# A fused attention and max-out MoE kernel: early pieces of the first copies, a new order of loads at the start, and one score tile per pair moved into the MoE's accumulator banks

## The chip, the cores and the metric

One core of one Trainium2 chip. The metric is the device time of one launch in microseconds (us), lower is better.

## The reference

Block-wise causal attention (blocks of 64 tokens) on 8 batches, 8 heads, 576 tokens, head size 64; its result, 4608 tokens of 512, goes through two matrices of 512x1024, an elementwise maximum, and one of 1024x512.

```python
def _attn_ref(q, k, v):                      # each (8, 8, 576, 64)
    scores = scale * np.matmul(q, k.transpose(0, 1, 3, 2))
    mask = block_i >= block_j                # blocks of 64 tokens
    scores = np.where(mask, scores, -1000000000.0)
    attn = np.exp(scores - max); attn = attn / sum
    return np.matmul(attn, v)

def _moe_ref(x, w1, w2, w_out):              # x (4608, 512)
    g = np.maximum(x @ w1, x @ w2)           # (4608, 1024)
    return g @ w_out
```

## The kernel before

The program is scheduled by hand: each engine runs its instructions in the order in which they are written. Attention works on pairs of heads, two pairs to a group, 16 groups; 64-row matmuls for scores and transposes run two at a time on the halves of the array (in the trace the two of a pair start 0.003 us apart). MoE matmuls of 128 rows fill in between: `fill(n)` issues n of them. Accumulators lie in PSUM: the pool `ps_s` has two score buffers of two banks each, the pool `ps_m` four single banks, which h units, y units, attention output (`av`) and transposes share in rotation. An h unit makes 128 columns of g for up to 512 tokens, a y unit the final output of 128 tokens; `x_out` transposes the attention output into the MoE's input.

```python
def h_unit(i, f):                            # 8 matmuls, two banks of ps_m
    for w_sb in (w1_sb, w2_sb):
        pt = ps_m.tile([P, SPAN], FP32, name="ps_h", tag="m")
        for c in range(NDM):
            nc.tensor.matmul(pt[:, :w], w_sb[:, c, ...], xT[:, c, t0:t0 + w], ...)
            if c == NDM - 1:
                if not ph:
                    nc.vector.tensor_copy(out=h1[:, :w], in_=pt[:, :w])       # frees bank 1
                else:
                    nc.vector.tensor_max(g[:, f, m:m + w], h1[:, :w], pt[:, :w])  # frees bank 2
            yield                            # (bookkeeping cut)

def tile_0(p):                               # tile_1, tile_2 alike: 2 halves x 512 columns
    u = ps_s.tile([P, 2, 512], FP32, name="ps_s", tag="s")
    scores(p, u, 0, 0, 0, 512)
    return lambda: (exp(p, u, 512, 0), mask(p, 0))
# ... cut ...
for g in range(GPB, NG):                     # the steady loop, as before
    region(tile_0(a), tile_1(a))             # block of 64-row matmuls 1
    for p, tiles in ((a, lambda: (tile_2(a), tile_0(b))), (b, lambda: (tile_1(b), tile_2(b)))):
        fill(hi); av_with(p - LAG, lo)       # MoE and attention output
        copy_out = t_pair(p); outs = tiles() # blocks 2 and 3, with transposes
        copy_out(); region(*outs)
```

Loads of weights and v are issued by GpSimd, which also casts group 2's q and k; loads of q and k are issued by the sync engine.

The softmax here doesn't subtract the row's maximum and nothing guards it: scores larger than these inputs give would overflow.

Of the kernel before, what the change touches and what calls it, by code (L numbers as in the profile page):

```python
# [8 lines left out]
FP32 = mybir.dt.float32  # L9
BF16 = mybir.dt.bfloat16  # L10
AF = mybir.ActivationFunctionType
# [3 lines left out]
def kernel(  # L15
# [10 lines left out]
    nc = tc.nc  # L26
# [84 lines left out]
    def load_qk(g, queues, gated=False):  # L111
        b, u = divmod(g, GPB)
        for nm, src, queue in (("q", q, queues[0]), ("k", k, queues[1])):
            if queue is None:
                continue
            raws[nm, g] = t = raw.tile([P, 2, RPP * D], FP32, name=f"{nm}raw")
            if gated:
                nc.gpsimd.memset(t[:, 0, :1], 0.0)
            queue.dma_start(
                out=t[:],  # L120
                in_=src[b, 4 * u:4 * u + 4].rearrange(
                    "(s h) (p t) d -> (h p) s (t d)", h=2, t=RPP),
            )

    def cast(nm, g, parts):
        t = raws.pop((nm, g)).rearrange("p s (t d) -> p t s d", d=D)
        qk_n[nm, g] = n = qkn.tile([P, RPP, 2, D], BF16, name=f"{nm}n")
        for copy, j0, j1 in parts:
            copy(out=n[:, j0:j1], in_=t[:, j0:j1])  # L129
# [12 lines left out]
    def load_w(f0, fw, which=(0, 1)):  # L142
        for i in which:
            dst, src = ((w1_sb, w1r), (w2_sb, w2r))[i]
            nc.gpsimd.dma_start(out=dst[:, :, f0:f0 + fw], in_=src[:, :, f0:f0 + fw])
# [11 lines left out]
    nc.vector.memset(zeros[:], 0.0)  # L157
    nc.scalar.activation(out=warm[:], in_=warm[:], func=AF.Exp)
    load_qk(1, (SP, SP))
    load_qk(2, (SP, None))  # L160
    make_identity(nc, ident)
    for r in range(NV):
        nc.vector.memset(vv_r[r][:, :, :, D:D + 1], 1.0)
# [9 lines left out]
    load_w(0, 256, (0,))  # L173
    cast("k", 1, ((pool, 0, RPP),))
    load_w(0, 256, (1,))
    load_qk(2, (None, SP), gated=True)


    done_tokens = [0]
# [88 lines left out]

    plan()
    steps = [(u, need, cost) for u, need, cost, n in units for _ in range(n)]  # L270
    at = [0]


# [4 lines left out]
            n += 1  # L278
        return int(total)

    def fill(n):
        while n > 0 and at[0] < len(steps) and steps[at[0]][1] <= done_tokens[0]:
            u, _, cost = steps[at[0]]
            next(u)
            n -= cost
            at[0] += 1


    def warm_up(n):
        pw = ps_m.tile([P, SPAN], FP32, name="ps_w", tag="m")  # L290
        for _ in range(n):
            nc.tensor.matmul(pw[:], zeros[:, :P], zeros[:], start=True, stop=True)  # L292
# [4 lines left out]
    def transposes(nm, g, copies):  # L297
        n = qk_n.pop((nm, g))
        pts = [ps_m.tile([P, RPP, NP], BF16, name=f"ps_{nm}T", tag="m") for _ in range(2)]
        for j in range(RPP):  # L300
            for i in range(2):
                r = slice(i * NP, (i + 1) * NP)
                nc.tensor.transpose(  # L303
                    pts[i][:, j, :], n[r, j].rearrange("p s d -> p (s d)"), ident[r, r],
                )

        def copy_out(which=(0, 1)):
            for i in which:
                t = (qT_r if nm == "q" else kT_r)[(2 * g + i) % NT]
                copies[i](  # L310
                    out=t[:, :S].rearrange("q (p j) -> q p j", j=RPP),
                    in_=pts[i].rearrange("q j p -> q p j"),
                )
        return copy_out

# [11 lines left out]
    def pad_keys(p):  # L327
        nc.gpsimd.tensor_copy(
            out=kz_r[p % NT].rearrange("p (a c) -> p a c", c=BLK)[:, 0:3:2],
            in_=kT_r[p % NT][:, S - 3 * BLK:].rearrange("p (a c) -> p a c", c=BLK)[:, 0:3:2],  # L330
        )


    def corner_scores(p, ps, col):
# [25 lines left out]
    def burst_p(p):  # L360
        burst(p, ((0, 0, QCUT), (1, P, QCUT - P)), 0)

    def burst_q1(p):
        burst(p, ((0, QCUT, 320), (1, QCUT, 192)), 384)

    def burst_q2(p):
        burst(p, ((1, 448, P), (2, QCUT, 320), (4, 512, BLK)), 896)
# [4 lines left out]
    def masks_p(p, eng=None):  # L372
        for a in (0, 256):
            mask(p, a, eng)
# [34 lines left out]
    def region(*tiles):  # L409
        for out in tiles:  # L410
            out()

    def av(p, ts):
        b, hp = divmod(p, HP)
        vv = vv_r[b % NV]
        a = aT_r[p % NA]
        n = len(ts)
        h0 = hp // 2 * 4 + hp % 2
        if p % 2 == 0 and ts[0] == 0:
            xps[p // 2] = xpool.tile([P, NCH, 2, 2, D], BF16, name="xp")  # L420
        xp = xps[p // 2]
        po = ps_m.tile([P, n, 2, D + 1], FP32, name="ps_o", tag="m")
        n_mm = 2 * sum(t + 1 for t in ts)
        mm = 0
        for gi, t in enumerate(ts):
            for hh in range(2):
                for c in range(t + 1):
                    a0 = a_col(p, c, t)
                    nc.tensor.matmul(  # L429
                        po[:, gi, hh, :], a[:, hh, a0:a0 + P], vv[:, c, h0 + 2 * hh, :],  # L430
                        start=(mm == 0), stop=(mm == n_mm - 1),
                    )
                    mm += 1
        rec = small.tile([P, 3, 2, 1], FP32, name="rec")
        nc.vector.reciprocal(rec[:, :n, :, 0], po[:, :, :, D])  # L435
        nc.vector.tensor_mul(  # L436
            xp[:, ts[0]:ts[0] + n, :, p % 2], po[:, :, :, :D],
            rec[:, :n].to_broadcast([P, n, 2, D]),
        )

    def x_out(g, t0=0, t1=NCH):
        b, u = divmod(g, GPB)
        xp = xps[g]
        n = t1 - t0
        n_odd = min(t1, NCH - 1) - t0
        pe = ps_m.tile([P, 2, n, BLK], BF16, name="ps_xe", tag="m")
        po = ps_m.tile([P, 2, n_odd, BLK], BF16, name="ps_xo", tag="m")
        for s in range(2):
            for t in range(t0, t1):
                src = xp[:, t, s].rearrange("p a d -> p (a d)")  # L450
                nc.tensor.transpose(pe[:, s, t - t0, :], src[:BLK], ident[:BLK, :BLK])  # L451
                if t < NCH - 1:
                    nc.tensor.transpose(po[:, s, t - t0, :], src[BLK:], ident[BLK:, BLK:])
        dst = xT[:, 2 * u:2 * u + 2, b * S + t0 * P:b * S + t1 * P].rearrange(
            "p s (t h w) -> p s t h w", h=2, w=BLK)
        nc.vector.tensor_copy(out=dst[:, :, :, 0], in_=pe[:])  # L456
        nc.vector.tensor_copy(out=dst[:, :, :n_odd, 1], in_=po[:])
        if u == GPB - 1:
            done_tokens[0] = min(b * S + t1 * P, (b + 1) * S)

# [37 lines left out]
        return lambda: [f() for f in outs]  # L498


    warm_up(16)
    cq = transposes("q", 0, (dve, act))
    ck = transposes("k", 0, (act, dve))
    cq((0,))
    ck((0,))
    cq((1,))
    ck((1,))
    cast("q", 1, ((dve, 0, RPP),))
    burst_p(0)
    masks_p(0)  # L510
    burst_p(1)
    warm_up(2)
    masks_p(1)
    for c in range(2, NCH):
        load_v(0, c)
    load_w(256, 256)
    cq = transposes("q", 1, (dve, dve))
    burst_q1(0)
    ck = transposes("k", 1, (dve, dve))
    for i in range(2):  # L520
        cq((i,))
        ck((i,))
    load_w(512, 512)
    warm_up(3)
    burst_p(2)
    av(0, [0, 1])
    burst_q3(0)
    warm_up(2)
    burst_p(3)
    masks_p(2, nc.vector)  # L530
    av(1, [0, 1])
    masks_p(3, nc.vector)
    burst_q2(0)
    av(2, [0, 1])
    warm_up(2)
    burst_q1(1)
    av(3, [0, 1])
    x_out(0, 0, 2)
    warm_up(2)
    cast("q", 2, ((pool, 0, RPP),))  # L540
    masks_q(0)
    cast("k", 2, ((pool, 0, RPP),))
    burst_q2(1)
    x_out(1, 0, 2)
    warm_up(2)
    burst_q3(1)
    masks_q(1)
    for c in range(3):
# [39 lines left out]

    for g in range(GPB, NG):
        a, b = 2 * g, 2 * g + 1  # L590
        if x_due:
            x_out(x_due.pop())
        n = fill_of(g)
        region(tile_0(a), tile_1(a))
        if g == GPB:
            av(3, [2, 3, 4])
            fill(5)
            x_out(1, 2, NCH)
            n = fill_of(g)
        lo, hi = max(3, n // 18), n * 2 // 9  # L600
        for p, tiles in ((a, lambda: (tile_2(a), tile_0(b))), (b, lambda: (tile_1(b), tile_2(b)))):
            fill(hi)
            if g > GPB:
                av_with(p - LAG, lo)
            else:
                fill(lo)
            copy_out = t_pair(p)
            outs = tiles()
            copy_out()
            region(*outs)  # L610
            if p % 2 and g + 1 < NG:
                pad_keys(p + 1)
                pad_keys(p + 2)
            pool_work(p)
        if g > GPB:
            x_due.append(g - 1)
        fill(n - 2 * (lo + hi))
    for p in range(NPAIR - LAG, NPAIR):
        if x_due:
            x_out(x_due.pop())  # L620
# [40 lines left out]
```

## Time and profile before

| | before |
|---|---|
| time, median (4 runs, one of them slow) | 283.05 us (282.59 to 287.41) |
| TensorE busy | 96% |
| steady group | 15.0 us, three 64-row blocks |
| first h matmul | 18.09 us |

First, GpSimd's timeline (columns: start, duration, engine, line, what, how many in a row, and in brackets the idle time ahead with what ended it):

```profile
10.25 0.75 POOL L145 DMA_DIRECT2D w_sb<-in_moe_w_dram  x1
...
11.73 2.44 POOL L133 DMA_DIRECT2D vv<-in_v_dram  x3
14.15 3.01 POOL L145 DMA_DIRECT2D w_sb<-in_moe_w_dram  x4
17.20 1.14 POOL L129 CAST qn<-qraw 128x1152 bf16<-128x1152 f32 x1
```

It starts the cast of group 2's q at 17.20. Second, TensorE's timeline shows where the loop proper begins: the first full score tile, at 27.06.

```profile
27.06 0.61 PE L321 MATMUL ps_s<-qT,kT 64*128 64x512 bf16 x6
```

### The profile page before, as it was taken

Reading aid. Unit: us, or ns where it says so; the run is one execution under the profiler, and the core shown is the slowest. Engines: PE = TensorE matmul, PEld = TensorE weight load, DVE = VectorE, ACT = ScalarE, POOL = GpSimd, SP = SyncE. Lnnn points to the kernel's source line nnn. Section 1 sums busy time; section 2 is a strip of 40 time slices with the busy share of each in tenths; the row PEclk is TensorE's granted clock in tenths of the full one; section 3 lists DMA queues with packets and bytes.
Section 4 is the critical chain, followed back from the end, with each engine's and each line's share of the span. In section 5 each row is a group of like instructions: output and inputs, shape, how many; then the busy total and the mean of one; then the engine's idle time right before and its main releaser. Section 6 shows DMA issues by size and latency. Waiting matters only on the chain.

```text
span 280.4 us, 7767 instructions
## 1 busy us (share of the span) xinstructions
PE 269.3 (96%) x3208; PEld 151.5 (54%) x3253; DVE 185.7 (66%) x386; ACT 139.6 (50%) x194; POOL 107.7 (38%) x271
## 2 busy tenths in 40 slices
PE   7699999999999999999999999999999999999995
PEld 2356766655556455555555554646455644444543
DVE  5967879668887676767667576757655766365430
ACT  3786577667664664655647374664653000100112
POOL 2996446764654625164344625371120000000000
PEclk9999999999999999999999999999999999999999
DMA  7999999979934994479266866175301111111114
GB/s 261 263 219 220 187 244 273 250 148 189 210 42 153 154 156 78 178 82 239 49 208 77 219 75 196 52 81 50 67 5 49 49 54 40 39 75 40 73 41 150
DMA packets 55940, 36.68 MB, mean 131 GB/s; under 512 B 38752, under 2 KB 43232, under 8 KB 55904
## 3 DMA queue, kind: packets, MB, share of 16 engines
q0 software_dynamic: 41728, 7.87, 35.0%
q1 hardware_dynamic: 13760, 27.66, 28.8%
q10 hardware_dynamic: 416, 0.66, 0.7%
q8 instruction: 25, 0.41, 0.6%
q14 instruction: 11, 0.09, 0.1%
HBM read 34.60 MB, written 9.44 MB: 157 GB/s over the span
## 4 chain that ended last, share of the span: by engine, by line
PE 91%; DMA 4%; issue 2%; ACT 1%; DVE 1%; POOL 0%; ACTq 0%
PE ps_h L197 43%; PE ps_y L215 22%; PE ps_o L429 11%; PE ps_s L321 8%; DMA vv<-in_v_dram 2%; PE ps_xe L451 2%; PE ps_qT L303 2%; DMA qraw<-in_q_dram 2%; PE ps_kT L303 2%; ACT aT L345 1%; PE ps_s L339 1%; PE ps_y L231 1%; PE ps_w L292 1%; DVE g L206 0%; POOL vv L133 0%
## 5 line engine op out<-in xcount | busy, mean ns | idle before, releaser
L197 PE MATMUL ps_h<-xT,w_sb 128*128 128x512 bf16 (+3 forms) x605 | 136.2, 357 | 1.7 <-issue 0.3
L345 ACT ACTIVATE aT<-ps_s 128x1024 bf16<-128x1024 f32 (+2 forms) x100 | 96.2, 996 | 17.2 <-PE ps_s L321 16.2
L197 PEld LDWEIGHTS <-w_sb 128*128 128x128 bf16 x640 | 57.8, 98 | 57.4 <-issue 8.1
L204 DVE CAST h<-ps_h 128x512 bf16<-128x512 f32 (+3 forms) x80 | 50.9, 637 | 28.9 <-PE ps_h L197 26.7
L215 PE MATMUL ps_y<-wo_sb,g 128*128 128x512 bf16 x273 | 65.5, 379 | 2.1 <-PE ps_s L321 1.3
L206 DVE TENSOR_TENSOR g<-h,ps_h 128x512 bf16<-128x512 bf16 (+3 forms) x80 | 50.6, 632 | 12.0 <-PE ps_h L197 10.5
L350 POOL MEMSET aT<- 64x128 bf16 x124 | 22.3, 199 | 92.7 <-ACT aT L345 91.3
L221 ACT COPY y<-ps_y 128x512 f32<-128x512 f32 x31 | 18.1, 584 | 70.3 <-PE ps_y L215 56.5
L429 PEld LDWEIGHTS <-aT 128*128 128x128 bf16 x960 | 37.3, 98 | 14.1 <-issue 1.3
L215 PEld LDWEIGHTS <-g 128*128 128x128 bf16 x280 | 26.8, 98 | 30.4 <-issue 1.1
L429 PE MATMUL ps_o<-vv,aT 128*128 128x65 bf16 x960 | 39.9, 194 | 0.3 <-DMA vv<-in_v_dram 0.3
L133 POOL DMA_DIRECT2D vv<-in_v_dram x40 | 33.7, 847 | 0.5
L436 DVE TENSOR_TENSOR xp<-ps_o,rec 128x256 bf16<-128x256 f32 (+1 forms) x64 | 31.4, 491 | 2.2
L321 PE MATMUL ps_s<-qT,kT 64*128 64x64 bf16 (+6 forms) x344 | 31.6, 279 | 1.1 <-ACT kT L310 0.7
L435 DVE RECIPROCAL rec<-ps_o 128x4 f32<-128x4 f32 (+1 forms) x64 | 12.0, 188 | 20.6 <-PE ps_o L429 18.9
L310 ACT COPY qT<-ps_qT 128x576 bf16<-128x576 bf16 x15 | 9.6, 638 | 29.4 <-PE ps_qT L303 29.4
L187 POOL COPY g<-g 128x512 bf16<-128x512 bf16 x8 | 4.9, 611 | 38.3 <-DVE g L206 38.2
L129 POOL CAST kn<-kraw 128x1152 bf16<-128x1152 f32 x15 | 17.3, 1151 | 5.2 <-DMA kraw<-in_k_dram 5.1
L129 POOL CAST qn<-qraw 128x1152 bf16<-128x1152 f32 (+1 forms) x15 | 16.5, 1099 | 7.0 <-DMA qraw<-in_q_dram 6.9
L456 DVE COPY xT<-ps_xe 128x640 bf16<-128x640 bf16 (+2 forms) x18 | 8.2, 453 | 15.7 <-PE ps_xe L451 14.9
L310 ACT COPY kT<-ps_kT 128x576 bf16<-128x576 bf16 x15 | 9.6, 638 | 15.0 <-PE ps_kT L303 15.0
L321 PEld LDWEIGHTS <-kT 64*128 64x128 bf16 x344 | 13.2, 95 | 6.6 <-issue 2.8
(44 smaller groups left out, 144.5 us busy)
## 6 DMA issues: line engine op xcount, KB each, us to landing
qraw<-in_q_dram SPq DMA_DIRECT2D x16, 576.0 KB, 4.1
out_dram<-y SPq DMA_DIRECT2D x35, 256.0 KB, 2.1
kraw<-in_k_dram SPq DMA_DIRECT2D x15, 576.0 KB, 5.4
vv<-in_v_dram POOLq DMA_DIRECT2D x32, 128.0 KB, 5.3
w_sb<-in_moe_w_dram POOLq DMA_DIRECT2D x4, 256.0 KB, 6.6
w_sb<-in_moe_w_dram POOLq DMA_DIRECT2D x2, 512.0 KB, 10.7
wo_sb<-in_moe_w_out_dram POOLq DMA_DIRECT2D x2, 512.0 KB, 11.8
kraw<-in_k_dram ACTq DMA_DIRECT2D x1, 576.0 KB, 5.4
```

The lines of the kernel that those rows point to most:

```text
L129: copy(out=n[:, j0:j1], in_=t[:, j0:j1])
L133: nc.gpsimd.dma_start(out=vv_r[b % NV][P - rows:, c, :, :D], in_=v[b, :, c * P:c * P + rows, :].rearrange("h p d -> p h d"),)
L197: nc.tensor.matmul(pt[:, :w], w_sb[:, c, f * P:(f + 1) * P], xT[:, c, t0:t0 + w], start=(c == 0), stop=(c == NDM - 1),)
L204: nc.vector.tensor_copy(out=h1[:, :w], in_=pt[:, :w])
L206: nc.vector.tensor_max(g[:, f, m:m + w], h1[:, :w], pt[:, :w])
L215: nc.tensor.matmul(py[:], g[:, f, s * P:(s + 1) * P], wo_sb[:, f, :], start=(f == 0), stop=(f == NFF - 1),)
L310: copies[i](out=t[:, :S].rearrange("q (p j) -> q p j", j=RPP), in_=pts[i].rearrange("q j p -> q p j"),)
L321: nc.tensor.matmul(ps[:, hh, col:col + w], kT[r, k0:k0 + P], qT[r, q0:q0 + w], start=True, stop=True,)
L345: nc.scalar.activation(out=aT_r[p % NA][:, :, a0:a0 + w], in_=ps[:, :, :w], func=AF.Exp, scale=scale,)
L350: (eng or nc.gpsimd).memset(aT_r[p % NA][BLK:, :, a0:a0 + BLK], 0.0)
L429: nc.tensor.matmul(po[:, gi, hh, :], a[:, hh, a0:a0 + P], vv[:, c, h0 + 2 * hh, :], start=(mm == 0), stop=(mm == n_mm - 1),)
L436: nc.vector.tensor_mul(xp[:, ts[0]:ts[0] + n, :, p % 2], po[:, :, :, :D], rec[:, :n].to_broadcast([P, n, 2, D]),)
```

## The change

Two ideas. At the **start**, the columns of the transposed q and k that the first scores need are copied first (`LOW`), the rest behind (`HIGH`), partly on ScalarE; the weight blocks are loaded ahead of the rest of v, the last weights in two blocks of 256 columns instead of one of 512; group 2's q is loaded later, with its k. In the **loop**, tile 0 of each pair goes into two of the four MoE banks, so that all three tiles of a pair fit into one 64-row block: two blocks a group instead of three, and fewer switches between 64-row and 128-row mode. For that, `fill` gets a second argument that runs MoE units to their end before a block, so that whole banks come free, and in the loop `x_out`'s even copy goes to ScalarE; neither is in the cut below.

```diff
-    load_qk(2, (SP, None))                  # group 2's q, early
...
-    load_qk(2, (None, SP), gated=True)
+    load_qk(2, (SP, SP), gated=True)
...
+    def tile_0m(p):
+        us = [ps_m.tile([P, 512], FP32, name="ps_s0", tag="m") for _ in range(2)]
+        for hh in (1, 0):
+            nc.tensor.matmul(us[hh][:], kT_r[p % NT][r, :P], qT_r[p % NT][r, :512], ...)
+        def out():
+            for hh in range(2):
+                nc.scalar.activation(out=aT_r[p % NA][:, hh, :512], in_=us[hh][:], func=AF.Exp, scale=scale)
...                                           # the start
-    cq((0,)); ck((0,)); cq((1,)); ck((1,))
+    cq((0,), LOW); ck((0,), LOW); ck((1,), LOW); cq((1,), LOW); cq((0,), HIGH) ...
+    load_w(256, 256)
     for c in range(2, NCH):
         load_v(0, c)
-    load_w(256, 256)
...
-    burst_q1(0)                              # ahead of group 1's k transposes
...
-    load_w(512, 512)
+    load_w(512, 256)
+    load_w(768, 256)
...
+    x_out(0, 0, 2, (act, act))               # was behind the later scores, on VectorE
+    burst_q1(0)                              # now behind x_out(0)
...                                           # the loop, pair a; pair b has t_pair first
+                out1 = tile_1(a); out0 = tile_0m(a); out2 = tile_2(a)
+                copy_out = t_pair(a)
+                out0(); out1(); copy_out(); out2()
```

More of the change, by code (lines that the diff above doesn't have):

```diff
@@ L270 @@
     steps = [(u, need, cost) for u, need, cost, n in units for _ in range(n)]
+    inside = [j % (NDM if n > NFF or n == 2 * NDM and u.__name__ == "h_unit" else NFF) > 0
+              for u, _, _, n in units for j in range(n)]
     at = [0]
@@ L279, in ready, with fill @@
         return int(total)
-    def fill(n):
-        while n > 0 and at[0] < len(steps) and steps[at[0]][1] <= done_tokens[0]:
+    def fill(n, whole=False):
+        while at[0] < len(steps) and steps[at[0]][1] <= done_tokens[0]:
+            if n <= 0 and not (whole and inside[at[0]]):
+                break
             u, _, cost = steps[at[0]]
@@ L305, in transposes, with copy_out @@
                 )
-        def copy_out(which=(0, 1)):
+        def copy_out(which=(0, 1), part=(0, NP), copy=None):
+            p0, p1 = part
             for i in which:
                 t = (qT_r if nm == "q" else kT_r)[(2 * g + i) % NT]
-                copies[i](
-                    out=t[:, :S].rearrange("q (p j) -> q p j", j=RPP),
-                    in_=pts[i].rearrange("q j p -> q p j"),
+                (copy or copies[i])(
+                    out=t[:, p0 * RPP:p1 * RPP].rearrange("q (p j) -> q p j", j=RPP),
+                    in_=pts[i][:, :, p0:p1].rearrange("q j p -> q p j"),
                 )
@@ L331, in pad_keys @@
         )
+    def tile_0m(p):
+        us = [ps_m.tile([P, 512], FP32, name="ps_s0", tag="m") for _ in range(2)]
+        for hh in (1, 0):
+            r = slice(hh * D, (hh + 1) * D)
+            nc.tensor.matmul(
+                us[hh][:], kT_r[p % NT][r, :P], qT_r[p % NT][r, :512], start=True, stop=True)
+        def out():
+            for hh in range(2):
+                nc.scalar.activation(
+                    out=aT_r[p % NA][:, hh, :512], in_=us[hh][:], func=AF.Exp, scale=scale)
+            mask(p, 0)
+        return out
     def corner_scores(p, ps, col):
@@ L439, in av, with x_out @@
         )
-    def x_out(g, t0=0, t1=NCH):
+    def x_out(g, t0=0, t1=NCH, copies=(dve, dve)):
         b, u = divmod(g, GPB)
@@ L455, in x_out @@
             "p s (t h w) -> p s t h w", h=2, w=BLK)
-        nc.vector.tensor_copy(out=dst[:, :, :, 0], in_=pe[:])
-        nc.vector.tensor_copy(out=dst[:, :, :n_odd, 1], in_=po[:])
+        copies[0](out=dst[:, :, :, 0], in_=pe[:])
+        copies[1](out=dst[:, :, :n_odd, 1], in_=po[:])
         if u == GPB - 1:
@@ L498, in t_pair @@
         return lambda: [f() for f in outs]
+    LOW = (0, -(-QCUT // RPP))
+    HIGH = (LOW[1], NP)
     warm_up(16)
@@ L503 @@
     ck = transposes("k", 0, (act, dve))
-    cq((0,))
-    ck((0,))
-    cq((1,))
-    ck((1,))
+    cq((0,), LOW)
+    ck((0,), LOW)
+    ck((1,), LOW)
+    cq((1,), LOW)
+    cq((0,), HIGH)
     cast("q", 1, ((dve, 0, RPP),))
@@ L510 @@
     masks_p(0)
+    cq((1,), HIGH)
+    ck((0,), HIGH)
     burst_p(1)
+    ck((1,), HIGH)
     warm_up(2)
     masks_p(1)
+    load_w(256, 256)
     for c in range(2, NCH):
         load_v(0, c)
-    load_w(256, 256)
-    cq = transposes("q", 1, (dve, dve))
-    burst_q1(0)
-    ck = transposes("k", 1, (dve, dve))
-    for i in range(2):
-        cq((i,))
-        ck((i,))
-    load_w(512, 512)
-    warm_up(3)
-    burst_p(2)
-    av(0, [0, 1])
-    burst_q3(0)
-    warm_up(2)
-    burst_p(3)
-    masks_p(2, nc.vector)
-    av(1, [0, 1])
-    masks_p(3, nc.vector)
-    burst_q2(0)
-    av(2, [0, 1])
-    warm_up(2)
-    burst_q1(1)
-    av(3, [0, 1])
-    x_out(0, 0, 2)
-    warm_up(2)
-    cast("q", 2, ((pool, 0, RPP),))
+    cq = transposes("q", 1, (dve, act))
+    ck = transposes("k", 1, (dve, dve))
+    cq((0,), LOW)
+    cq((1,), LOW)
+    ck((0,), LOW)
+    ck((1,), LOW)
+    cq((0,), HIGH, act)
+    cq((1,), HIGH, dve)
+    load_w(512, 256)
+    load_w(768, 256)
+    warm_up(2)
+    burst_p(2)
+    ck((0,), HIGH, act)
+    av(0, [0, 1])
+    masks_p(2, nc.vector)
+    burst_p(3)
+    av(1, [0, 1])
+    ck((1,), HIGH, act)
+    masks_p(3, nc.vector)
+    warm_up(1)
+    av(2, [0, 1])
+    x_out(0, 0, 2, (act, act))
+    warm_up(1)
+    av(3, [0, 1])
+    burst_q1(0)
+    warm_up(1)
+    x_out(1, 0, 2, (dve, dve))
+    burst_q2(0)
+    warm_up(1)
+    cast("q", 2, ((pool, 0, RPP),))
+    fill(2)
+    burst_q3(0)
     masks_q(0)
     cast("k", 2, ((pool, 0, RPP),))
+    burst_q1(1)
+    fill(1)
     burst_q2(1)
-    x_out(1, 0, 2)
-    warm_up(2)
+    fill(1)
     burst_q3(1)
@@ L590 @@
         a, b = 2 * g, 2 * g + 1
-        if x_due:
-            x_out(x_due.pop())
         n = fill_of(g)
-        region(tile_0(a), tile_1(a))
-        if g == GPB:
-            av(3, [2, 3, 4])
-            fill(5)
-            x_out(1, 2, NCH)
-            n = fill_of(g)
-        lo, hi = max(3, n // 18), n * 2 // 9
-        for p, tiles in ((a, lambda: (tile_2(a), tile_0(b))), (b, lambda: (tile_1(b), tile_2(b)))):
-            fill(hi)
+        fill(0, True)
+        for p in (a, b):
+            if p == a and x_due:
+                x_out(x_due.pop(), copies=(act, dve))
+                n = fill_of(g)
+            if p == a:
+                out1 = tile_1(a)
+                out0 = tile_0m(a)
+                out2 = tile_2(a)
+                copy_out = t_pair(a) if g > GPB else (lambda: None)
+                out0()
+                out1()
+                copy_out()
+                out2()
+            else:
+                copy_out = t_pair(b)
+                out1 = tile_1(b)
+                out0 = tile_0m(b)
+                out2 = tile_2(b)
+                copy_out()
+                out1()
+                out0()
+                out2()
+                if g + 1 < NG:
+                    pad_keys(p + 1)
+                    pad_keys(p + 2)
+            pool_work(p)
+            if g == GPB and p == a:
+                av(3, [2, 3, 4])
+                fill(5)
+                x_out(1, 2, NCH)
+                t_pair(a)()
+                n = fill_of(g)
+            lo = max(3, n // 18)
+            hi = max(0, n // 2 - lo)
             if g > GPB:
+                fill(hi * 3 // 5)
                 av_with(p - LAG, lo)
+                fill(hi - hi * 3 // 5, True)
             else:
-                fill(lo)
-            copy_out = t_pair(p)
-            outs = tiles()
-            copy_out()
-            region(*outs)
-            if p % 2 and g + 1 < NG:
-                pad_keys(p + 1)
-                pad_keys(p + 2)
-            pool_work(p)
+                fill(lo + hi, True)
         if g > GPB:
             x_due.append(g - 1)
-        fill(n - 2 * (lo + hi))
     for p in range(NPAIR - LAG, NPAIR):
```

## The prediction

> **What bounds the kernel now.** I read the page's busy shares first, then the waits of TensorE, then the table by stretches, then the timeline of one steady group, and last the groups by shape for the durations.
>
> ```profile
> PE 269.3 (96%) x3208; PEld 151.5 (54%) x3253; DVE 185.7 (66%) x386; ACT 139.6 (50%) x194; POOL 107.7 (38%) x271
> ...
> PE 91%; DMA 4%; issue 2%; ACT 1%; DVE 1%; POOL 0%; ACTq 0%
> ```
>
> TensorE (PE) is busy 96% of the span and is 91% of the chain that ended last. Busy is not yet proof, so I ask for its waits:
>
> ```profile
> PE ps_y L215 <- PE ps_s L321: 1.3, 8, 0.2
> PE ps_w L292 <- DVE zeros L157: 1.2, 1, 1.2
> PE ps_qT L303 <- DVE qn L129: 0.9, 2, 0.5
> ```
>
> The longest total is 1.3 us, and that one is records missing from the trace (a gap of 0.16 us where one matmul of 0.216 us must stand). So from about 18 us on, when the first `ps_h` matmul runs, PE waits for nobody. The table by stretches (columns PE, PEld, DVE, ACT, POOL) agrees:
>
> ```profile
> 0.00:10.00 10.00, 7.04 (x61) 2.93 (x62) 6.77 (x21) 4.46 (x7) 4.53 (x11) 1.00 0.84 296
> 10.00:20.00 10.00, 8.86 (x151) 5.02 (x155) 7.58 (x24) 7.70 (x11) 9.73 (x18) 1.00 1.82 204
> ...
> 140.00:160.00 20.00, 19.68 (x235) 10.70 (x238) 12.83 (x26) 11.14 (x15) 10.75 (x23) 1.00 0.66 161
> ```
>
> Two things can therefore pay: less dead PE time before 18 us, and less PE time lost between kinds of matmul. One steady group lasts 15.0 us (x_out starts at 156.44 and again at 171.45). Its last 64-row block and what follows it (columns: start, duration, engine, line, what, how many in a row):
>
> ```profile
> 165.76 0.44 PE L303 MATMUL ps_kT<-ident,kn 64*128 64x64 bf16 x18
> 166.03 0.38 PE L321 MATMUL ps_s<-qT,kT 64*128 64x64 bf16 x4
> ...
> 166.31 0.36 PE L321 MATMUL ps_s<-qT,kT 64*128 64x320 bf16 x4
> 166.60 2.76 PE L197 MATMUL ps_h<-xT,w_sb 128*128 128x512 bf16 x11
> 169.20 1.89 PE L215 MATMUL ps_y<-wo_sb,g 128*128 128x512 bf16 x8
> 170.93 0.59 PE L197 MATMUL ps_h<-xT,w_sb 128*128 128x512 bf16 x2
> 171.45 0.20 PE L451 MATMUL ps_xe<-ident,xp 64*128 64x64 bf16 x1
> ```
>
> Starts are to be compared, not durations: eight ps_y take 170.93-169.20 = 1.73, so 0.216 us each. Two ps_h from 170.93 end at 171.36, but the first transpose starts at 171.45: going from 128-row to 64-row mode costs 0.095. On the way back, the pairs of 320 and 128 columns take 0.137+0.056 from 166.31, that is to 166.50, and ps_h starts at 166.60: 0.095 again. A group has three such blocks, six switches, 0.57 us; everything else runs at its streaming rate.
>
> **What the Trainium skill says.** "TensorEngine Tiling (Array Packing)", Tiling Modes, Key Properties: changing the tiling mode drains the array. The trace agrees, 0.095 us each way. "TensorE: Matmul & The Clock Gate", Back-to-back issue gap: N/2.4+2.5 ns, 216 ns for 512 columns; the trace has 0.216 (and not the 131 ns that the same section gives for a sustained stream). "PSUM — Partial Sum Buffer", Specifications: 8 banks of 2 KiB per partition. The two score buffers of 4 KiB take four and the four MoE buffers the other four, so a score tile placed in two MoE banks takes them from h, y, av and transposes. The TensorE page, Architectural detail, has VectorE and ScalarE as strict FIFOs, so a bank comes free only in the order of their queues; the timeline shows both starting their work in program order.
>
> **Part 1, the steady loop: what it removes.** By the order of the built programs, 64-row blocks fall from 61 to 47: one per group for 14 groups. 14 x 2 x 0.095 = **2.7 us less**.
>
> **What it adds.** Tile 0 of each pair now sits in two of the four MoE banks. The program's waits say on whom: its first half waits for the h1 copy (VectorE cast) of the last h unit, its second half for the maximum of that same unit, whose last matmul is the last instruction ahead of the block. Before the change, no 64-row block waited on the latest two banks. How soon can that maximum end?
>
> ```profile
> 168.54 0.69 DVE L204 CAST h<-ps_h 128x512 bf16<-128x512 f32 x1 [0.17 <-PE ps_h L197]
> 169.40 0.69 DVE L206 TENSOR_TENSOR g<-h,ps_h 128x512 bf16<-128x512 bf16 x1 [0.17 <-PE ps_h L197]
> ```
>
> The h units' boundaries are at 168.336 and 169.199 (starts of the next matmul); VectorE begins 0.20 later and takes 0.69. With about 0.06 to let PE go (a transpose at 24.33 waited for a copy that ended at 24.27), the bank is free 0.95 us after the unit. Set t=0 at the end of the last full-array matmul.
> - Block B (k transposes, tiles 1, 0, 2): switch 0.095, transposes 0.265, tile 1 (64 and 448 columns in pairs) 0.22: tile 0 could run at 0.58, its second half runs at 0.95. **Lost 0.37.** Tile 2 0.25 and the switch follow: MoE resumes at 1.51. Its first bank (k copy on ScalarE, 0.64) is free by 1.3: no more lost.
> - Block A (x_out, tiles 1, 0, 2, q transposes): 0.095+0.30+0.22 = 0.61, so **0.33 lost** until 0.95; tile 0 ends at 1.16, tile 2 at 1.41, transposes at 1.68, switch 1.78. The first h bank there is the one tile 0 left, and waits for the new half exponential on ScalarE: result at 1.16+0.16, 512 columns. Its time I read off the rows by shape:
>
> ```profile
> L345 ACT ACTIVATE aT<-ps_s 128x1024 bf16<-128x1024 f32 x92 | 91.3, 1026 | 15.5 <-PE ps_s L321 14.6 <-ACT aT L401 0.5
> ...
> L345 ACT ACTIVATE aT<-ps_s 128x768 bf16<-128x768 f32 x4 | 3.1, 814 | 1.0 <-PE ps_s L321 1.0
> L345 ACT ACTIVATE aT<-ps_s 128x384 bf16<-128x384 f32 x4 | 2.0, 489 | 0.8 <-PE ps_s L321 0.6
> ```
>
> 0.85 ns a column over 0.16: 0.60 us (an estimate from these rows). It ends near 1.96, PE goes on at 2.02: **0.25 lost**.
>
> So a group gains 0.19 and loses 0.37+0.33+0.25 = 0.95: **+0.76 us**. Ten full groups give 7.6. The four others (320-column spans, whose maximum takes 0.49, and the last group without transposes) I put at 0.5 to 0.6 each, 2.2. Together **+9.8 us**. All of it is on the path, as PE is the bound and no later slack takes it up. Two exponentials of 0.60 for one of 1.03 add 0.17 x 28 = 5 us to ScalarE, which is half idle; x_out's even copy goes from VectorE (0.49) to ScalarE. Neither is on the path beyond what is counted.
>
> **Part 2, the first 30 us.** Copies of 261 and 315 columns replace 576; q1's and k1's four VectorE copies (0.75 each, 10.6 to 13.35) become three early pieces ready by about 11.4, so the scores of pairs 2 and 3 start near 11.3 and 11.9 instead of 12.1 and 13.9. The first h matmul should come at 15.9 to 16.4 instead of 18.09, **some 2 us earlier**. But ScalarE takes over pieces: ten copies of about 0.4 instead of two of 0.64, some 2 us more net of overlap, on the engine that is busiest with exponentials there (7.70 of 10 us above). The exponentials of the later columns queue behind: after the first h, the blocks up to the q transposes of group 2 wait for score buffers and run with 12 h matmuls between them instead of 4. I put PE at those scores (18.63 before) at 19.2 to 19.7, with eight more 256-column matmuls (8 x 0.109 = 0.87 us) done. That cancels to within a microsecond: **0, give or take 1**. GpSimd also holds four w loads that each wait for an older load to land, ahead of group 2's casts (at 17.2 before, perhaps 18.5): another way to give it back. Weights of later columns arrive sooner; PE lost only little to them.
>
> **Sum:** 283.2 - 2.7 + 12.5 + 0 = 293; I take **292.5 us**.
>
> **Rivals.**
> 1. The intent holds: the waits hide and the start pays 2 us: 278.5. For it: no stall of PE today, VectorE is only two thirds busy. Against it: the wait is for one certain instruction, which cannot start before its matmul ends; a free engine does not shorten it.
> 2. The start pays its 2 us and the loop loses as worked out: 290.5.
> 3. ScalarE falls behind: its order per block (x copy, two halves, tile 1, q copy, tile 2) frees the q copy's bank only at about 4.0, against a need at 4.4 in block A. If its instructions run 10% slower in this order, another 0.3 a group: 297.
> 4. A moderate loop loss: banks free earlier than I read, half the stalls: 287, within 2%.
>
> **Range and chances.** The stalls follow from measured durations and the built order, so most weight is on a loss of 6 to 12 us; rival 4 and a good start make the lower end. 285 to 296.5. Faster by over 2% (under 277.6) would need nearly no stall: 0.05. Within 2% (to 288.9): 0.23. Slower: 0.72.
>
> **What would show it.** After: PE waits of about 0.35 us, some 27 times, on the h1/maximum line just ahead of the second half of tile 0, and some 13 of 0.25 on the new half exponential; group period 15.7 to 15.8 instead of 15.0; first h at about 16 with the scores of group 2 no earlier. I am wrong if the period is 15.0 or less, or if the first 30 us do over 2 us more work.

## More of the kernel before

At the start, group 2's q was loaded as the fifth transfer, at 2.26 us.

The granted clock is full from end to end.

## The result, and the profile after

The changed kernel takes **299.22 us** (median of 4 runs, 297.45 to 300.17); before, 283.05. The ratio is **1.057** (95% interval 1.0505 to 1.0634). Executions over 1.5% slower than the fastest of the same kernel are left out of the means. Ratios here are from the runs of the same rounds, so not quite the ratio of the medians. It is slower, as predicted, but by 16 us where 9 were predicted, and outside the range. The page of the kernel after, its busy line, its clock by fortieths of the span, and its chain:

```profile
PE 279.9 (94%) x3207; PEld 151.9 (51%) x3248; DVE 180.7 (61%) x374; ACT 150.0 (50%) x242; POOL 109.1 (37%) x274
...
PEclk9996999999999999999999999999999999999999
...
PE 83%; DMA 6%; ACT 3%; issue 3%; POOL 2%; DVE 2%; SPq 0%; ACTq 0%; POOLq 0%; DVEq 0%
```

In the chain TensorE's share fell from 91 to 83%, and DMA's rose from 4 to 6, ScalarE's from 1 to 3 and GpSimd's from 0 to 2; one slice has a clearly lowered clock. The waits of TensorE (total, times, longest):

```profile
PE ps_qT L306 <- POOL qn L129: 2.3, 3, 1.0
PE ps_h L196 <- DMA w_sb<-in_moe_w_dram: 2.2, 1, 2.2
PE ps_h L196 <- ACT aT L347: 2.1, 9, 0.2
```

The third is the loop's and was predicted (0.25 us at the first h behind the half exponential; some 13 of them, where the list has 9 and one more at a y matmul). The second and the first of the three in the top row (at 24.28) are the start's; the other two of that row come later (at 47.38 and 70.94).

**The loop after.** One steady 64-row block B (k transposes and three tiles), TensorE and then VectorE:

```profile
118.14 0.38 PE L325 MATMUL ps_s<-qT,kT 64*128 64x64 bf16 x4
118.36 0.72 PE L342 MATMUL ps_s<-qT,kT 64*128 64x512 bf16 x2
...
119.27 1.04 PE L196 MATMUL ps_h<-xT,w_sb 128*128 128x512 bf16 x4
```

```profile
117.97 0.69 DVE L205 TENSOR_TENSOR g<-h,ps_h 128x512 bf16<-128x512 bf16 x1 [0.17 <-PE ps_h L196]
```

The two halves of tile 0 (L342) would run side by side, but their own records start at 118.360 and 118.710, 0.35 apart. The second half needs the bank that the maximum at 117.97 reads, and that ends at 118.66. The last h matmul ended at 117.77 (its start, 117.554, plus 0.216): the second half starts 0.94 us after it, and the block lasts 1.50. The list of waits does not show this wait, because the first half's record, 0.38 us long, covers it. In block A the MoE's first matmul then waits for the half exponential as well:

```profile
127.44 0.38 PE L196 MATMUL ps_h<-xT,w_sb 128*128 128x512 bf16 x1 [0.23 <-ACT aT L347]
```

Block A lasts 2.06 us and the period of a group is 15.75 (x_out's first transpose starts at 109.725 and again at 125.478).

**The start after.** GpSimd's timeline, to be held against the one of before:

```profile
10.52 0.75 POOL L145 DMA_DIRECT2D w_sb<-in_moe_w_dram  x1
...
12.03 1.48 POOL L145 DMA_DIRECT2D w_sb<-in_moe_w_dram  x2
13.49 2.47 POOL L133 DMA_DIRECT2D vv<-in_v_dram  x3
15.91 1.54 POOL L145 DMA_DIRECT2D w_sb<-in_moe_w_dram  x2
20.57 0.74 POOL L145 DMA_DIRECT2D w_sb<-in_moe_w_dram  x1 [3.12 <-DMA w_sb<-in_moe_w_dram]
22.29 0.74 POOL L145 DMA_DIRECT2D w_sb<-in_moe_w_dram  x1 [0.97 <-DMA w_sb<-in_moe_w_dram]
23.08 1.14 POOL L129 CAST qn<-qraw 128x1152 bf16<-128x1152 f32 x1
```

Its last two weight loads each wait, 3.12 and 0.97 us, for an older weight load to land, and everything behind them waits too: the cast starts at 23.08, 5.9 us later than before, though q itself had landed at 18.60. The semaphores in the trace tell which load is waited for. GpSimd's loads signal on eight semaphores in turn, and a load first waits for its own to be free, so the twelfth waits for the fourth (landed 20.29) and the thirteenth for the fifth (22.01). Before, eleven loads stood ahead of the cast, and those waited for had landed in time; splitting the last weights makes it thirteen. And TensorE:

```profile
16.77 0.60 PE L196 MATMUL ps_h<-xT,w_sb 128*128 128x256 bf16 x4
...
20.34 0.39 PE L196 MATMUL ps_h<-xT,w_sb 128*128 128x256 bf16 x2 [2.21 <-DMA w_sb<-in_moe_w_dram]
...
24.28 0.66 PE L306 MATMUL ps_qT<-ident,qn 64*128 64x64 bf16 x18 [0.97 <-POOL qn L129]
```

The first h does come early, at 16.77, but the next waits 2.21 us for the second matrix's first block, which landed at 20.29 (16.32 before; landing times are my reading of the trace's DMA records). In the table by stretches (PE, PEld, DVE, ACT, POOL busy, then clock, DMA share, GB/s):

```profile
0.00:10.00 10.00, 6.74 (x61) 2.88 (x62) 6.66 (x23) 4.19 (x9) 4.26 (x11) 1.00 0.98 256
...
20.00:30.00 10.00, 8.69 (x110) 5.16 (x112) 3.60 (x9) 4.58 (x6) 8.10 (x16) 0.66 1.79 176
```

In the first 10 us 256 GB/s were moved against 296 before, as group 2's q is no longer among them; it moved into the stretch where weights and v compete. From 20 to 30 TensorE looks busy, but at a clock of 0.66: for 6.83 us from 21.10 its matmuls took double the time (six h matmuls from 24.87 to 26.27, 0.23 each, against 0.109 at the full clock). Counting work: the first full score tile comes at 34.27 with 40 h matmuls done, against 27.06 with 30. Ten h matmuls of 256 columns are 1.1 us (0.109 each), so the start is **6.1 us** late.

### The profile page after: what moved, and what is told of

Read it like the earlier page. It is cut to its first block, busy times and chain, and to the rows that moved or that the text cites. A ratio compares the mean times of both kernels' runs of the same rounds, so it can differ in the third digit from the quotient of the medians.

```text
span 297.7 us, 7823 instructions
## 1 busy us (share of the span) xinstructions
PE 279.9 (94%) x3207; PEld 151.9 (51%) x3248; DVE 180.7 (61%) x374; ACT 150.0 (50%) x242; POOL 109.1 (37%) x274
## 4 chain that ended last, share of the span: by engine, by line
PE 83%; DMA 6%; ACT 3%; issue 3%; POOL 2%; DVE 2%; SPq 0%; ACTq 0%; POOLq 0%; DVEq 0%
PE ps_h L196 40%; PE ps_y L214 20%; PE ps_o L448 10%; PE ps_s L325 4%; PE ps_s L342 4%; DMA w_sb<-in_moe_w_dram 3%; ACT aT L347 3%; DMA kraw<-in_k_dram 3%; PE ps_kT L306 2%; PE ps_xe L470 2%; POOL qn L129 1%; PE ps_qT L306 1%; PE ps_y L230 1%; DVE xp L455 1%; DVE g L205 0%
## 5 line engine op out<-in xcount | busy, mean ns | idle before, releaser
L196 PE MATMUL ps_h<-xT,w_sb 128*128 128x512 bf16 (+3 forms) x615 | 138.2, 360 | 5.8 <-DMA w_sb<-in_moe_w_dram 2.2
L364 ACT ACTIVATE aT<-ps_s 128x1024 bf16<-128x1024 f32 (+2 forms) x72 | 71.5, 1000 | 11.1 <-PE ps_s L325 10.9
L214 PE MATMUL ps_y<-wo_sb,g 128*128 128x512 bf16 x265 | 69.6, 379 | 1.1 <-ACT aT L347 0.2
L205 DVE TENSOR_TENSOR g<-h,ps_h 128x512 bf16<-128x512 bf16 (+3 forms) x80 | 50.6, 633 | 15.9 <-PE ps_h L196 13.5
L214 PEld LDWEIGHTS <-g 128*128 128x128 bf16 x280 | 24.6, 97 | 23.6 <-issue 0.6
L325 PE MATMUL ps_s<-qT,kT 64*128 64x128 bf16 (+5 forms) x288 | 32.1, 266 | 0.6 <-ACT kT L314 0.5
L347 ACT ACTIVATE aT<-ps_s 128x512 bf16<-128x512 f32 x56 | 30.5, 603 | 3.2 <-PE ps_s L342 2.0
L314 ACT COPY kT<-ps_kT 128x576 bf16<-128x576 bf16 (+2 forms) x18 | 10.6, 589 | 24.2 <-PE ps_kT L306 24.2
L342 PE MATMUL ps_s<-qT,kT 64*128 64x512 bf16 x56 | 19.3, 375 | 0.2
L314 DVE COPY qT<-ps_qT 128x576 bf16<-128x576 bf16 (+2 forms) x18 | 12.4, 690 | 11.5 <-PE ps_qT L306 11.3
L475 ACT COPY xT<-ps_xe 128x640 bf16<-128x640 bf16 (+1 forms) x13 | 8.7, 667 | 20.1 <-PE ps_xe L470 20.0
L129 POOL CAST qn<-qraw 128x1152 bf16<-128x1152 f32 (+1 forms) x15 | 16.5, 1098 | 6.0 <-DMA qraw<-in_q_dram 5.9
```

Of the source, the lines that this page charges most:

```text
L129: copy(out=n[:, j0:j1], in_=t[:, j0:j1])
L196: nc.tensor.matmul(pt[:, :w], w_sb[:, c, f * P:(f + 1) * P], xT[:, c, t0:t0 + w], start=(c == 0), stop=(c == NDM - 1),)
L214: nc.tensor.matmul(py[:], g[:, f, s * P:(s + 1) * P], wo_sb[:, f, :], start=(f == 0), stop=(f == NFF - 1),)
L325: nc.tensor.matmul(ps[:, hh, col:col + w], kT[r, k0:k0 + P], qT[r, q0:q0 + w], start=True, stop=True,)
L342: nc.tensor.matmul(us[hh][:], kT_r[p % NT][r, :P], qT_r[p % NT][r, :512], start=True, stop=True)
L347: nc.scalar.activation(out=aT_r[p % NA][:, hh, :512], in_=us[hh][:], func=AF.Exp, scale=scale)
```

## The experiments

Thirteen kernels; all gave correct results. In the table, "against before" is (ratio - 1) times before's median of the same rounds (282.5 to 283).

| run | what it is | median us | ratio | against before, us |
|---|---|---|---|---|
| after | the whole change | 299.22 | 1.0570 | +16.1 |
| e_loop | changed loop, start of before | 293.54 | 1.0383 | +10.8 |
| e_start | changed start, loop of before | 289.69 | 1.0232 | +6.6 |
| e_q2early | after, group 2's q loaded early again | 295.65 | 1.0455 | +12.9 |
| e_w512 | after, last weights in one block | 297.30 | 1.0525 | +14.8 |
| e_vfirst | after, rest of v ahead of weights | 299.09 | 1.0597 | +16.9 |
| e_warm | after, 12 dummy matmuls more | 298.32 | 1.0545 | +15.4 |
| e_fix_all | after, all three loads undone | 294.96 | 1.0441 | +12.5 |
| e_start_q2 | e_start, q early again | 284.97 | 1.0082 | +2.3 |
| e_start_fix | e_start, all three loads undone | 284.15 | 1.0051 | +1.4 |
| e_fix_dve | e_start_fix, four copies on VectorE | 284.97 | 1.0071 | +2.0 |
| e_fix_q1 | e_start_fix, pair 0's later scores early | 285.07 | 1.0084 | +2.4 |
| e_fix_q1d | e_fix_q1, two copies on VectorE | 284.91 | 1.0070 | +2.0 |
| e_order | after, tile 0 last in its block | 297.26 | 1.0516 | +14.6 |

### Which half costs what

My theory here: the loop costs what was worked out and the start the rest. Rival: the loop costs it all and the start's lag is caught up later.

```diff
 # e_loop: the start (order, copies, loads) is that of before; the loop stays changed
 # e_start: the other way round
```

> The start of the kernel before (its loads, copies and order up to the masks of pair 1) with the changed steady loop. Theory: the loop costs what was worked out, about 0.75 us a group, so the time is 283 + 9.5 to 11 = 293 to 294 us, group period 15.7 to 15.8 us, TensorE clock 1.00 throughout. Rival (most of the loss comes from the start, and the loop period of 15.75 is partly its after-effect): under 290 us.

> The changed start with the steady loop of the kernel before. Theory: the start loses about 6 us (TensorE waits for the second weight block until 20.3 us, then its clock is halved for some 6 us), so 288.5 to 290 us, with the wait and a granted clock near 0.6 in the window from 20 to 30 us again. Rival (the start is only unlucky together with the new loop): 283 to 284 us.

Measured +10.8 (1.0356 to 1.0411) and +6.6 (1.0191 to 1.0273). Their sum, 17.4, is the whole 16.1 within the intervals. The theory holds: the loop alone is what the prediction said, and the start, which it put at nothing, loses 6.6.

### The loads, one at a time

```diff
 # e_q2early
+    load_qk(2, (SP, None))                  # fifth transfer again, as before
-    load_qk(2, (SP, SP), gated=True)
+    load_qk(2, (None, SP), gated=True)
 # e_w512
-    load_w(512, 256)
-    load_w(768, 256)
+    load_w(512, 512)
 # e_vfirst: load_w(256, 256) behind the load_v loop instead of ahead of it
```

> The changed kernel with one thing undone: group 2's q is again loaded without a gate right behind group 1's k. Theory (q and k of group 2 issued at 11.4 us share the DMA engines with the second weight block): that block lands near 16.5 instead of 20.3 us, TensorE does not wait for it, the clock stays at 1.00, and the time falls by 5 to 6 us to about 293.5 us. Rival (GpSimd held by its weight loads, which wait for older loads, or ScalarE's extra copies, cause the loss): less than 2 us gained, over 297 us.

> The changed kernel with the last two weight blocks loaded as one of 512 columns per matrix, as in the kernel before: two DMA issues fewer. Theory (GpSimd stops at its last two weight issues until older loads have landed, 4.1 us in all, and group 2's casts stand behind them): those waits vanish, the cast of q starts when q lands, near 19 us instead of 23.1, and the time falls by 1 to 2.5 us, to about 297.5 us; TensorE still waits some 2 us for the second weight block. Rival (the casts are late because of the DMA alone): under 0.7 us.

> The changed kernel with v's rest loaded ahead of the second pair of weight blocks, as before the change. Theory (the weights moved forward share the DMA engines with the second weight block of the first pair and delay it): that block lands 1 to 2 us sooner than 20.3 and the time falls by 1 to 2 us. Rival (only group 2's q and k delay it): no gain, within 0.7 us of 299.2.

q early alone gave back 3.2 us, between the theory and its rival: the second weight block landed at 19.24, not at 16.5, TensorE still waited 0.8 us for it, and GpSimd was still held behind weight loads. The single block of 512 columns makes it eleven loads again and let GpSimd reach its cast at 17.58. That gave back 1.3, as expected, though within the interval of after (1.8 us either way). The expected wait for the second weight block did not show (it landed at 18.18 here); another did:

```profile
PE ps_o L448 <- DMA vv<-in_v_dram: 2.4, 2, 1.4
```

v first gave nothing, as its rival said: the cast stayed at 22.40 and TensorE waited 2.5 us for it. The weight block landed at 18.18 there too, but that shows no effect of v's place: with the loads up to 15.6 us as in after, it landed at 18.18 (e_w512), 19.37 (e_start), 19.76 (e_warm) and 20.29 (after), so one trace says little about one edit. What the three runs do show is that mending one place left a wait at another.

> The changed kernel with its loop left as it is and all three changes of the loads undone (group 2's q loaded early again, the rest of v ahead of the second weight blocks, the last weights as one block of 512 columns). Its start's early copies and new order stay. If the parts add up (loop +10.8 from one run, start without load changes +1.4 from another, before 282.7): 294.9 us, ratio 1.043; first cast of group 2's q at about 17.1 us, no TensorE wait for weights or for that cast, no stretch at half clock. Then the loads account for some 4 to 5 of the 6.5 us that the start lost. Rival (one load is enough, as group 2's q early alone gave 295.65 and ratio 1.0455): 295.5 or more.

```diff
 # e_fix_all: the three edits above together, on the whole changed kernel
```

Measured 1.0441 (1.0411 to 1.047), as expected from adding up; the cast is back at its old time and the wait for weights is gone:

```profile
17.11 1.14 POOL L129 CAST qn<-qraw 128x1152 bf16<-128x1152 f32 x1
```

There and in e_start_fix below the second weight block landed at 16.65 and 17.37, ahead of all of the above. So the three loads together account for 16.1 - 12.5 = 3.6 us with the changed loop. With the loop of before:

> The changed start with group 2's q loaded early, and the steady loop of the kernel before: the early copies and the order of the weights alone. Theory: without the DMA collision the start is worth nothing to 2 us, 281 to 283.5 us. Rival (the pieces on ScalarE or the waits of GpSimd cost time by themselves): 285 us or more.

> All three load changes undone (q of group 2 early, v's rest first, 512-column blocks), with the early copies and the new order of the start kept, and the loop of the kernel before. Theory (the loads alone made the start slow): first h matmul near 16.5 us, no wait for weights, cast of q near 17.3 us, 280.5 to 282.5 us, at or a little under the kernel before. Rival (the pieces on ScalarE and the deferred columns eat the gain): 283 to 285 us.

e_start_q2 missed: 284.97 instead of at most 283.5. Its second weight block landed at 18.01, its cast came at 20.43, and the clock was halved from 10.9 to 17.7 us. e_start_fix came to 284.15 (1.0029 to 1.0072), the range of its rival: the loads are worth 6.6 - 1.4 = 5.2 us there. The two figures, 3.6 and 5.2, agree within their intervals (about 2 and 1.3 us either way); and what is left, the early copies and the new order, **costs** 1.4 us instead of gaining 2.

### The halved clock

```diff
     burst_q1(1)
+    warm_up(12)
```

> The changed kernel with twelve idle matmuls (2.6 us of zeros) put where TensorE waits for the second weight block; nothing else is touched, so that block lands at about 20.3 us as before. Theory (the halved clock of 6.8 us comes from that idle time and costs by itself): the clock stays at 1.00 and the time falls by 1 to 2.5 us, to about 297.5 us. Rival (the slow clock only fills time in which TensorE would wait for GpSimd's cast anyway): no gain, 299 us.

The clock between 20 and 30 us stayed full, but part of the stretch from 10 to 20 was halved instead, and the time fell by 0.7, within the intervals, where 1 to 2.5 had been expected. So this run does not settle the clock's share. The four executions of after took 297.45, 298.89, 299.54 and 300.17 us at mean clocks of 1.000, 0.993, 0.988 and 0.983, so some 1 to 2 us of the 16.1 may go with the clock, and the one at the full clock is still 14.4 us above before. Not every kernel shows this (the slowest execution of e_q2early, 296.80, has 0.999), and which of the two causes the other is not shown.

### What is left of the start without the loads

My theory: in the changed order pair 0's later scores stand behind the first x_out, so ScalarE loses an exponential's slot and pays later. The two kernels' ScalarE, before first, then e_start_fix:

```profile
10.81 1.02 ACT L345 ACTIVATE aT<-ps_s 128x1024 bf16<-128x1024 f32 x1 [0.46 <-PE ps_s L321]
```

```profile
15.90 5.87 ACT L365 ACTIVATE aT<-ps_s 128x1024 bf16<-128x1024 f32 x7 [0.41 <-PE ps_s L326]
```

Before, that exponential runs at 10.81; in the new order seven run back to back from 15.90 to 21.77, and the scores of group 2 come at 20.32 instead of 18.63, with 8 more h matmuls done (0.87 us): 0.8 us late. Three attempts to take the cause away:

```diff
 # e_fix_dve: the two late k pieces and x_out(0)'s two copies
-    ck((0,), HIGH, act); ck((1,), HIGH, act); x_out(0, 0, 2, (act, act))
+    ck((0,), HIGH, dve); ck((1,), HIGH, dve); x_out(0, 0, 2, (dve, dve))
 # e_fix_q1
     cq = transposes("q", 1, (dve, act))
+    burst_q1(0)
     ck = transposes("k", 1, (dve, dve))
...
-    burst_q1(0)
 # e_fix_q1d: e_fix_q1 with the two late k pieces on dve
```

> The kernel with the changed start, all load changes undone and the loop of before (284.15 us, 1.0051), with one more edit: three of the five ScalarE pieces of group 1's and x_out(0)'s copies, that is the two late k pieces and the two x_out copies (four instructions, about 1.6 us of ScalarE), go to VectorE instead. If ScalarE's queue, which runs its exponentials back to back from 15.9 to 21.8 us there, is what eats the early copies' gain: ScalarE is ahead by 1 to 1.6 us, the scores of group 2 come at about 19 instead of 20.3, and the time is 282.5 to 283.2 (ratio 0.999 to 1.002). Rival (the order itself, with x_out ahead of the later columns' scores, costs it): 284 or more, ratio unchanged at 1.005.

> The kernel with the changed start, all load changes undone and the loop of before (284.15 us, 1.0051), with one instruction group moved: pair 0's scores of the later columns (four matmuls and one exponential of 1024 columns) go back to where the kernel before has them, right behind the transposes of group 1's q, instead of behind the first x_out. If the remaining 1.4 us come from this deferral (in the kernel before ScalarE runs that exponential at 10.81, in a gap; in the changed order seven exponentials run back to back from 15.90 to 21.77 and the scores of group 2 come at 20.32 instead of 18.63): ScalarE's run of exponentials shortens by 1 us, the scores of group 2 come at about 19.3, and the time is 282.5 to 283.3 (ratio 0.999 to 1.002). If the early copies are worth their intended 2 us, even 281.5. Rival (the seven exponentials are not what bounds it): unchanged, 1.005.

> As the one before it, with the two late pieces of group 1's k copied on VectorE instead of ScalarE as well (0.44 us each; x_out's copies stay on ScalarE). If ScalarE is then still the limit: another 0.3 to 0.8 us, ratio 0.997 to 1.000. Rival (VectorE's queue, which holds the normalising that x_out waits for, becomes the limit, as when four copies went there): ratio 1.003 or more.

All three missed, at 1.0071, 1.0084 and 1.0070: none is better than e_start_fix. In e_fix_dve, ScalarE stood idle from 14.4 to 16.9, as x_out now waited for VectorE and the scores stand behind x_out in TensorE's order. In e_fix_q1, the exponential took its early slot, and the early copy that should have gone ahead of it stood behind (ScalarE, then TensorE):

```profile
9.89 1.76 ACT L365 ACTIVATE aT<-ps_s 128x768 bf16<-128x768 f32 x2
11.55 0.70 ACT L315 COPY qT<-ps_qT 128x261 bf16<-128x261 bf16 x2
```

```profile
12.29 1.01 PE L296 MATMUL ps_w<-zeros 128*128 128x512 bf16 x2 [1.45 <-ACT qT L315]
```

The traces of e_fix_dve and e_fix_q1 also hold 3.41 us of halved clock (from 15.74 and 12.30); that of e_fix_q1d holds none there, and it is no faster. My theory that the deferred exponential is by itself the cause falls. What the runs show is that the early pieces and the exponentials want the same engine, in order, between 9 and 16 us, and that each order tried puts a wait in another place. Which order would make the early pieces pay stays open; none of these did.

### Is it the maximum that holds the block?

```diff
-                out1 = tile_1(b); out0 = tile_0m(b); out2 = tile_2(b)
+                out1 = tile_1(b); out2 = tile_2(b); out0 = tile_0m(b)
 # and the same for pair a
```

> The changed kernel with one thing moved: in each pair's block tile 0 (the tile in the two MoE banks) is issued to TensorE last, after tile 2, instead of between tiles 1 and 2. Exponentials stay in the same order. My theory (the loss per group is TensorE waiting for the maximum of the last h unit, and in block A then for the half exponential that frees the first MoE bank): in block B 0.25 us of tile 2 moves ahead of the wait, so the wait falls from 0.37 to about 0.1 and the block from 1.50 to about 1.25 us; in block A the wait for the bank remains but tile 0 now starts its exponential about as late as before, so block A stays near 2.05. Over 14 groups about -3.5 us: ratio to the kernel before about 1.045 (295.5 us), period 15.5. Rival (what costs is the number of banks taken from h, y and transposes, not the order): no change, 1.057, period 15.75.

Block B in e_order, TensorE, then VectorE, then ScalarE:

```profile
115.84 0.44 PE L306 MATMUL ps_kT<-ident,kn 64*128 64x64 bf16 x18
...
116.59 0.47 PE L342 MATMUL ps_s<-qT,kT 64*128 64x512 bf16 x2
117.11 1.24 PE L196 MATMUL ps_h<-xT,w_sb 128*128 128x512 bf16 x5
```

```profile
115.95 0.69 DVE L205 TENSOR_TENSOR g<-h,ps_h 128x512 bf16<-128x512 bf16 x1 [0.17 <-PE ps_h L196]
```

```profile
116.42 0.64 ACT L314 COPY kT<-ps_kT 128x576 bf16<-128x576 bf16 x1 [1.62 <-PE ps_kT L306]
```

The last h matmul ended at 115.748 and the second half of tile 0 starts at 116.688: **0.94 us again**, though tile 2 now runs ahead of it. The order does not move it; the maximum, which ends at 116.64, does. What is saved is only what came behind: the MoE goes on after 1.37 us instead of 1.50. Block A stays at 2.06 (123.217 to 125.276), the period falls from 15.75 to 15.61, and 14 groups at 0.14 make 2.0; the times give 16.1 - 14.6 = 1.5 us, within after's interval, where I had expected 3.5. The late half (0.216) and the switch (0.095) after 0.94 would make the expected 1.25. What makes it 1.37 is ScalarE's k copy: it ends at 117.06, the MoE's first matmul waits for ScalarE's semaphore, which comes at 117.07, and starts at 117.115. The prediction had that bank free by 1.3, too early to matter in its order; here it is the next wait. The rival, that order does not matter at all, would have left the block at 1.50.

No version beat the kernel before, and the runs give no hint of one: the changed loop loses by itself, and the changed start never gained.

## Why the prediction was right or wrong

**Right: the loop.** The step that 64-row blocks would wait for the last h unit's maximum held to a few hundredths: block B 1.50 (predicted 1.51), block A 2.06 (2.02), period 15.75 (15.76). One slip in its sums: block A's exponential adds up to 1.92 (1.16 + 0.16 + 0.60), not to the 1.96 that it writes; the trace has its end at 2.01. The four shorter groups took somewhat more than the 2.2 us allowed for them: 10.8 - 10 x 0.75 = 3.3. Predicted +9.8, measured +10.8 by e_loop. Rival 3, ScalarE falling behind for good, is not needed: the full groups' measured loss is the sum of the two blocks' losses. Running units to their end and x_out's copy on ScalarE came with the loop and were not tried apart.

**Wrong: Part 2, the start.** The prediction's term was "0, give or take 1"; e_start measured +6.6. The failing step is the sentence "Weights of later columns arrive sooner; PE lost only little to them", and with it "group 2's casts (at 17.2 before, perhaps 18.5)". The second matrix's first block, which TensorE needed next, landed at 20.29, 4 us later than before, and cost a wait of 2.21 us; the casts came at 23.08. The prediction weighed the orders of the engines and gave no landing time for any load. But q of group 2 (issued at 11.40) and the two blocks ahead of v (12.03 and 12.76) were in flight together with that block (10.52). With the three load changes undone it landed at 16.65 to 17.37 and the cast came at 17.11 (e_fix_all), and the time fell by 3.6 (e_fix_all) to 5.2 us (e_start_fix); how this divides among the three is not shown. The prediction did name GpSimd's waits for older loads, but at some 1.3 us instead of 5.9.

**Half right: the early copies.** The first h came at 16.77 (predicted 15.9 to 16.4), and "ScalarE takes over pieces" and the exponentials queueing behind were foreseen as cancelling it. With the loads undone the residue is +1.4 us (e_start_fix; interval 0.8 to 2.0), at the edge of the term's "give or take 1": the scores of group 2 came at 20.32 where 19.2 to 19.7 was predicted (22.70 with the changed loads). Why they are late was not settled.

**In the sum** the prediction said +9.3 with a start of 0; the runs give 10.8 for the loop and 5.3 (16.1 - 10.8) to 6.6 (e_start) for the start. With that start the middle would have been 298 to 299.

## What to carry to other kernels

When a change moves loads, list for each consumer the transfers in flight ahead of or beside its own, not just the order of issue: a load that held up nothing where it stood (group 2's q in the first 10 us) can, together with others, cost several microseconds once it is moved next to weights that are needed at once, and an engine that both issues loads and casts hands such a delay on. Count the loads ahead of a cast as well: here the twelfth waited for the fourth. A buffer taken from a rotation is free when its last reader ends, so time the reader: here 0.94 us after the matmul, whatever the order inside the block. Score tiles in shared banks would need banks whose readers ended earlier; no run tried that.

## What the Trainium skill lacked or had wrong

- "DMA: Bandwidth & Descriptors", Anatomy of one DMA — SWDGE (gpsimd) path: its fit, 2.0 us plus bytes over 436e3, gives 3.2 us for a weight block of 512x256 float32 (0.52 MB as read; an estimate from that page). Issue to landing took 6.07 us before (10.25 to 16.32) and 9.77 after (10.52 to 20.29). The fit has no term for other loads in flight.
- "TensorE: Matmul & The Clock Gate", HAM oscillation: the rule given is no idle gaps above some 3.4 us. Here the clock was halved for 6.83 us with no TensorE wait longer than 2.21 us on its list, and in e_start_q2 from 10.9 to 17.7 with none longer than 1.2. The rule by itself does not cover these two.
- The same page, Back-to-back issue gap: 131 ns for a matmul of 512 columns in a sustained stream; the steady MoE stretches, before and after, show 216 ns.
- "TensorEngine Tiling (Array Packing)", Key Properties: says that a mode switch drains the array, not what that costs. The traces show 0.095 us each way (117.770 to 117.865 into block B of the kernel after).
